# Where the first nine weight chunks are added, how the first operands are loaded, and what the schedule counts for a transfer's issue

## The chip, the core and the metric

The kernel runs on one core of one Trainium2 chip. The metric is the device time of one execution in microseconds, the median of several runs. A core has four engines that compute here: PE (TensorE, matmuls; PEld is its loading of weights), DVE (VectorE), ACT (ScalarE) and POOL (GpSimd). SP (SyncE) only issues transfers, which 16 transfer engines carry out. Each engine takes its instructions from one queue, in order.

## The reference

Attention over 4 batches of 8 heads (576 positions, 64 per head), with a mask by blocks of 64 positions, feeds a first layer and that a second one. The inputs q, k and v are float32; the weights arrive as float64.

```python
scores = scale * np.matmul(q, k.transpose(0, 1, 3, 2))
mask = block_i >= block_j                      # blocks of 64
scores = np.where(mask, scores, -1000000000.0)
attn = np.exp(scores - np.max(scores, axis=-1, keepdims=True))
attn = attn / (np.sum(attn, axis=-1, keepdims=True) + 1e-09)
out = np.matmul(attn, v)
...
x = out.transpose(0, 2, 1, 3).reshape(2304, 512)
h = np.maximum(np.maximum(x @ w1, x @ w2), x @ w3)     # 512 -> 768
x = h @ w_out                                          # 768 -> 512
h = np.maximum(x @ w_in, 0.0)                          # 512 -> 2048
return h * h @ w_out                                   # 2048 -> 512
```

## The kernel before

**Attention.** Two heads make a pair, four pairs a batch, 16 pairs in all. The 576 positions are split into a first group of 256 query rows and a second of 320. For the first batch (pairs 0 to 3) the first group is done for all four pairs first, so that the first layer can begin early; its operands lie in one tile `zk` of 128x3x256: the queries of each head, padded with zeros to 128 rows (`z`, two slices), and the keys (`k`). `score_operands_f32` loads these three slices with three transfers, in the order z of head 0, k, z of head 1. For the tile of rows i (i is 0 or 1 in the first group) the names run: scores `sc_i`, masked with a memset; their row maxima `nm` (a reduction on DVE, then a small scaling); `P`, the exponentials with their row sums `sm`, on ACT; transposes `tp` on PE; a copy `ta` of them; the product with the values, `av`; reciprocals of the sums, spread by PE (`r`) and copied (`rs`); the scaled result split into a high part `xh` and a low part `xl`. The third group of operands belongs to pair 2, here called the third pair.

**Weights.** A weight of 64 bits is read as two 32-bit words, low and high, side by side in a tile `raw_w` of 128x512x2. `load_w_` makes a float32 `f_w` of one chunk (128x512) in steps: ACT scales the high words; ACT scales the low words to an integer; DVE shifts, then combines with the sign (`scalar_tensor_tensor`); GpSimd adds the two as 32-bit integers; ACT rounds to the high part `w1h`; DVE subtracts to get the low part `w1l`. The first layer has 18 chunks `w_c_i` (c is a block of 128 of its 768 columns, i one of w1, w2, w3), its second weights 6 (`wo1`). The chunks are numbered in the order in which they are recorded; `chunks` holds the names so far, the present one included. For a few chunks the place of `f_w` is the raw tile itself, and the rows then say `raw_w<-raw_w`.

**Products.** Each product of the first layer, `l`, is a sum of three matmuls: `xh` by `w1l`, `xl` by `w1h`, `xh` by `w1h`. The second layer does the same in another form, with weights written out to memory once and read back (`woh`, `wol`, `wq`).

**What sets the order.** All work is only recorded at first, in `Plan.note`. `Plan.issue` then goes through the recorded instructions with a clock of its own: for each engine it knows when the engine is free and when each instruction's operands are there, and it always takes the instruction that can start first (of several, the one of the lowest rank, then the earliest recorded), and writes it into that engine's queue. So the costs in `duration`, `transfer`, `SEM` and `LAP` set the order in every queue, SP's too. For a transfer the costs are: an issue holds SP for 60 ns, and the bytes pass a queue, at a fixed rate, that opens 1,500 ns after the issue. As all instructions are written by one helper, nearly all rows have line L187, and are told apart by the names of their tiles.

Of the kernel before, what the change touches and what calls it, by code (L numbers as in the profile page):

```python
# [17 lines left out]
ALU = mybir.AluOpType  # L18
# [6 lines left out]
NPAIR = H // 2  # L25
# [15 lines left out]
GA, GB = 256, 320  # L41
# [127 lines left out]
class Plan:  # L169
# [56 lines left out]
    def issue(self):  # L226

        ops, free, held, queue = self.ops, self.free, self.held, self.queue
        left = [0 for op in ops]
        users = [[] for _ in ops]  # L230
        for op in ops:
            for d in (*op.deps, *op.after):
                if d.end is None:
                    left[op.index] += 1
                    users[d.index].append(op)
        waiting = {e: {} for e in free}

        def offer(op):
            for e in op.engines:
                when = 0.0  # L240
                for d in op.deps:
                    when = max(when, d.end + ((SEM[d.engine] + (500 if e == 'pe' else 0)) if d.engine != e else 0))
                waiting[e][op.index] = when, shares_port(e, op)

        for op in ops:
            if not left[op.index]:
                offer(op)
        for _ in ops:
            best = None
            for e, w in waiting.items():  # L250
                if not w:
                    continue
                other = held["pool" if e == "dve" else "dve"] if e in held else 0.0
                start = {i: max(free[e], at, other if port else 0.0) for i, (at, port) in w.items()}
                t = min(start.values())
                i = min((i for i, s in start.items() if s <= t), key=lambda i: (ops[i].rank, i))
                if best is None or t < best[0]:
                    best = t, e, i
            t, e, i = best
            op = ops[i]  # L260
            op.engine = e
            length = duration(e, op) * SLOW[e]
            if e in held and waiting[e][i][1]:
                held[e] = t + length - HOLD[e]
            for other in op.engines:
                del waiting[other][i]
            if e == "sp":
                queue = max(t + 1500, queue) + transfer(op)
                op.end, free[e] = queue + 400, t + 60
            else:  # L270
                op.end = t + length
                free[e] = op.end - LAP[e]
            for tile in op.makes:
                tile.make()
            self.tc.keep_in_program_order(self.call(self.real[e], alias(e, op.name), op.args, op.kw))
            for u in users[i]:
                left[u.index] -= 1
                if not left[u.index]:
                    offer(u)
        self.ops, self.queue = [], queue  # L280
# [15 lines left out]
def width(x):  # L296
    return math.prod(x.area.shape[1:])


def alias(engine, name):  # L300
    return {"act": "copy", "dve": "tensor_copy"}.get(engine, name) if name in ("copy", "tensor_copy") else name


def shares_port(engine, op):
    if engine not in ("dve", "pool"):
        return False
    sources = [x for k, x in op.kw.items() if k.startswith("in") and isinstance(x, View) and not x.psum]
    if engine == "pool" or len(sources) > 1:
        return bool(sources)
    return bool(sources) and not op.kw["out"].psum and width(op.kw["out"]) % 2 == 0 and op.name != "tensor_reduce"  # L310
# [31 lines left out]
def transfer(op):  # L342
    x = next(v for v in op.views())
    return 128 * 4 * width(x) / 320.0


@with_exitstack
def fused_kernel(ctx: ExitStack, tc: tile.TileContext, z0, k0, qk, v, w123, wo1, win2, wo2, out):
    nc = Plan(tc)
    mm = nc.tensor.matmul  # L350

# [25 lines left out]
    def load_w(src, hi, lo, name):  # L377
        with nc.ranked(CFG["PC"]):
            load_w_(src, hi, lo, name)

    def load_w_(src, hi, lo, name, f=None):
        spare = SPARE[len(chunks)] if len(chunks) < len(SPARE) else "."
        chunks.append(name)
        if spare in "hl":
            both = m1.tile([128, 512, 3], U32, tag="h" + spare, name=f"raw_{name}").rearrange("p n t -> p (n t)")
            raw, f = both[:, :1024].rearrange("p (n t) -> p n t", t=2), both[:, 1024:].bitcast(F32)
        elif spare == "r":
            raw = at.tile([128, 512, 2], U32, tag="raw", bufs=CFG["RB"], name=f"raw_{name}")
            f = m1.tile([128, 512], F32, tag="xf", bufs=4, name=f"f_{name}")
        else:  # L390
            raw = m1.tile([128, 512, 2], U32, tag="wraw", bufs=2, name=f"raw_{name}")
            if f is None:
                f = m1.tile([128, 512], F32, tag="wf", bufs=2, name=f"f_{name}")
        nc.sync.dma_start(out=raw, in_=src.bitcast(U32).rearrange("p (n t) -> p n t", t=2))
        low, high = raw[:, :, 0], raw[:, :, 1]
        fi, qi = f.bitcast(I32), low.bitcast(I32)
        if pat(CFG["A1"] if len(chunks) <= 24 else CFG["A2"]):
            nc.vector.tensor_scalar(out=f, in0=high.bitcast(F32), scalar1=2.0 ** -112, scalar2=None, op0=ALU.mult)
        else:
            nc.scalar.activation(out=f, in_=high.bitcast(F32), func=AF.Copy, scale=2.0 ** -112)  # L400
        if pat(CFG["Q"] if len(chunks) <= 24 else CFG["Q2"]):
            nc.vector.tensor_scalar(out=qi, in0=low, scalar1=2.0 ** -29, scalar2=None, op0=ALU.mult)
        else:
            nc.scalar.activation(out=qi, in_=low, func=AF.Copy, scale=2.0 ** -29)
        nc.vector.tensor_scalar(out=fi, in0=fi, scalar1=3, scalar2=None, op0=ALU.logical_shift_left)
        nc.vector.scalar_tensor_tensor(out=fi, in0=high.bitcast(I32), scalar=-2 ** 31, in1=fi, op0=ALU.bitwise_and,
                                       op1=ALU.bitwise_or)
        if not CFG["HIS"]:
            nc.gpsimd.tensor_tensor(out=fi, in0=fi, in1=qi, op=ALU.add)
        if hi is None:  # L410
            return
        if pat(CFG["HI"]):
            nc.vector.tensor_copy(out=hi, in_=f)
        else:
            nc.scalar.copy(out=hi, in_=f)
        if CFG["HIS"] == 2:
            nc.gpsimd.tensor_tensor(out=fi, in0=fi, in1=qi, op=ALU.add)
        elif CFG["HIS"]:
            nc.gpsimd.tensor_tensor(out=qi, in0=fi, in1=qi, op=ALU.add)
            f = low.bitcast(F32)  # L420
        nc.vector.tensor_tensor(out=lo, in0=f, in1=hi.bitcast(F32), op=ALU.subtract)

    w1, wo1_t = {}, {}
    chunks = []
# [4 lines left out]
    def pat(p):  # L429
        return p > 0 and len(chunks) % p == 0 or p < 0 and len(chunks) % -p != 0  # L430
# [55 lines left out]
    def score_operands_f32(n, g):  # L486


        a, w = GROUPS[g] if n < NPAIR else (0, S)
        if n < NPAIR and g == 0:  # L490
            zk = at.tile([128, 3, GA], F32, tag="tb", bufs=2 * CFG["TB"][1], name=f"zk{n}")
            z, k = [zk[:, h] for h in range(2)], zk[:, 2]
        else:
            z = [at.tile([128, w], F32, tag=t, bufs=CFG["QB"][2 * (t == "kl")], name=f"z{n}_{t}") for t in ("qs", "kl")]
            k = at.tile([128, S], F32, tag="kh", bufs=CFG["QB"][1], name=f"k{n}")
        nc.sync.dma_start(out=z[0], in_=z0[n, :, 0, a:a + w])
        nc.sync.dma_start(out=k, in_=k0[n, :, :a + w])
        nc.sync.dma_start(out=z[1], in_=z0[n, :, 1, a:a + w])
        return [[(z[h], k)] for h in range(2)], None

    def value_operands(n, g):
# [279 lines left out]
    with nc.behind(marks[CFG["WO"]][0]), nc.ranked(2):  # L781
        for m in (m for q in range(NQ) for m in (q, q + NQ)):
            t = at.tile([128, 2, DM], F32R, tag="wos", name=f"wos{m}")
            load_w_(wo2[128 * m:128 * m + 128, :], t[:, 0], t[:, 1], f"wo_{m}")
            nc.sync.dma_start(out=wo_d[m], in_=t.bitcast(F32))
# [20 lines left out]
    def second_rows(q):  # L806
        f = forms_f[q] = w2p.tile([128, 8, 256], F32, tag="wqf", name=f"wqf{q}")
        load_w_(win2[q + NQ], None, None, f"wi_{q + NQ}", f[:, 0:2].rearrange("p i n -> p (i n)"))
# [240 lines left out]
```

## Time and profile before

| | |
|---|---|
| median of 3 runs | 888.12 us (883.44 to 889.05) |
| the profiled execution | 888.7 us, of which its span 886.9 us |
| mean granted clock of TensorE | 0.995 |
| PE busy | 864.2 us (97% of the span), 5464 matmuls |
| DVE busy | 601.1 us (68%) |
| ACT busy | 424.9 us (48%) |
| POOL busy | 104.0 us (12%), 94 instructions |
| moved by transfers | 157.73 MB, mean 178 GB/s |

The span is the time from the first to the last instruction on the core. An engine's busy time leaves out waits and the issuing of transfers. Matmuls are pipelined, so a full PE shows as busy all the time. [...] A row of a stage gives its start and end, its length, the busy time of each engine with the number of its instructions in brackets, the mean granted clock, the mean busy share of the transfer engines and the rate of the transfers.

### The profile page before, as it was taken

The numbers are of one execution on the slowest core, as the hardware profiler recorded it, in microseconds if no ns is written. First come the engines' busy times: TensorE is split into PE (matmuls) and PEld (weight loads), VectorE is DVE, ScalarE is ACT, GpSimd is POOL, SyncE is SP. The second block draws the span as 40 slices with busy tenths as digits, with TensorE's granted clock in tenths as the row PEclk, the third lists the DMA queues.
The fourth block names the chain that finished last, engine by engine and source line by source line (L and its number), as shares of the span: only waits on it lengthen the run. The fifth ranks groups of instructions, "written<-read, shape, count | busy, mean of one in ns | idle before, by whom it ended". The sixth has DMA issues, their size and how long they took to land.

```text
span 886.9 us, 14852 instructions
## 1 busy us (share of the span) xinstructions
PE 864.2 (97%) x5464; PEld 777.7 (88%) x5464; DVE 601.1 (68%) x1376; ACT 424.9 (48%) x1016; POOL 104.0 (12%) x94
## 2 busy tenths in 40 slices
PE   5899999999999999999999989999999999999997
PEld 4567799998999989899999979898999989999896
DVE  6998678878788988646557766546755457544543
ACT  6888667667688787544555231113211114211111
POOL 2233200000001111214442230000000000000000
PEclk9999999999999999999999999999999999999999
DMA  8745432232255563554656578454765536655221
GB/s 294 237 138 174 131 114 89 85 115 86 85 184 177 175 213 118 196 190 165 257 203 237 164 299 338 160 230 168 270 229 184 207 145 229 215 200 196 72 72 71
DMA packets 52056, 157.73 MB, mean 178 GB/s; under 512 B 8592, under 2 KB 16016, under 8 KB 48400
## 3 DMA queue, kind: packets, MB, share of 16 engines
q1 hardware_dynamic: 51984, 156.78, 50.5%
q8 instruction: 43, 0.70, 0.3%
q14 instruction: 29, 0.24, 0.1%
HBM read 124.26 MB, written 32.51 MB: 177 GB/s over the span
## 4 chain that ended last, share of the span: by engine, by line
PE 92%; DVE 2%; DMA 2%; ACT 2%; issue 0%; POOL 0%; SPq 0%; ACTq 0%; POOLq 0%; DVEq 0%
PE l L187 34%; PE acc L187 22%; PE ph_x L187 11%; PE ph_y L187 8%; PE av L187 5%; PE sc L187 5%; PE tp L187 4%; PE sc_t L187 2%; DMA raw_wi<-in_win 1%; PE tp_t L187 1%; DMA raw_wo<-in_wo 1%; DMA zk<-in_k 1%; PE r L187 0%; ACT P L187 0%; DVE f_wo L187 0%
## 5 line engine op out<-in xcount | busy, mean ns | idle before, releaser
L187 PE MATMUL acc<-woh,g 128*128 128x512 f32 x576 | 198.5, 395 | 0.0
L187 PE MATMUL l<-xh,w1l 128*128 128x256 f32 (+1 forms) x576 | 174.3, 303 | 0.9 <-DVE run L187 0.9
L187 PE MATMUL l<-xl,w1h 128*128 128x256 f32 (+1 forms) x576 | 172.2, 299 | 0.0
L187 PE MATMUL l<-xh,w1h 128*128 128x256 f32 (+1 forms) x576 | 172.2, 299 | 0.0
L187 ACT CAST g<-c 128x384 fp32r<-128x384 f32 x96 | 49.3, 513 | 220.8 <-DVE c L187 220.8
L187 PEld LDWEIGHTS acc<-woh,g 128*128 128x128 f32 x576 | 108.5, 189 | 19.4
L187 PE MATMUL acc<-wol,g 128*128 128x512 f32 x288 | 113.3, 393 | 0.0
L187 PEld LDWEIGHTS l<-xh,w1l 128*128 128x128 f32 x576 | 109.0, 189 | 4.1 <-issue 1.5
L187 PEld LDWEIGHTS l<-xl,w1h 128*128 128x128 f32 x576 | 109.1, 189 | 2.6 <-issue 1.7
L187 PEld LDWEIGHTS l<-xh,w1h 128*128 128x128 f32 x576 | 109.1, 189 | 1.9 <-issue 1.2
L187 PE MATMUL ph_x<-t,wq 128*128 128x384 f32 x432 | 87.7, 337 | 2.7 <-ACT p L187 2.7
L187 PEld LDWEIGHTS ph_x<-t,wq 128*128 128x128 f32 x432 | 77.4, 188 | 8.9 <-ACT p L187 3.1
L187 DVE TENSOR_TENSOR g<-c,g 128x384 fp32r<-128x384 f32 x96 | 53.6, 560 | 43.0 <-ACT g L187 42.6
L187 ACT ACTIVATE P<-sc,nm 128x128 f32<-128x128 f32 (+3 forms) x128 | 66.9, 530 | 9.9 <-DVE nm L187 8.4
L187 DVE TENSOR_TENSOR run<-l,run 128x256 f32<-128x256 f32 (+1 forms) x96 | 43.7, 455 | 27.9 <-PE l L187 26.3
L187 POOL TENSOR_TENSOR f_wo<-f_wo,raw_wo 128x512 int32<-128x512 int32 x22 | 29.8, 1357 | 276.5 <-DVE sm L187 180.3
L187 PEld LDWEIGHTS acc<-wol,g 128*128 128x128 f32 x288 | 54.3, 189 | 7.8
L187 PE MATMUL l<-hh,wo1l 128*128 128x256 f32 (+1 forms) x192 | 57.7, 306 | 2.2 <-DVE wo1l L187 2.1
L187 PE MATMUL ph_y<-b,wq 128*128 128x384 f32 x288 | 58.3, 337 | 0.0
L187 PE MATMUL l<-hl,wo1h 128*128 128x256 f32 (+1 forms) x192 | 57.5, 301 | 0.0
L187 PE MATMUL l<-hh,wo1h 128*128 128x256 f32 (+1 forms) x192 | 57.4, 300 | 0.0
L187 DVE TENSOR_REDUCE nm<-sc 128x2 f32<-128x256 f32 (+2 forms) x96 | 55.1, 588 | 0.8
(135 smaller groups left out, 1613.1 us busy)
## 6 DMA issues: line engine op xcount, KB each, us to landing
wq<-wq_d SPq DMA_DIRECT2D x20, 1792.0 KB, 8.6
wq_d<-wq SPq DMA_DIRECT2D x8, 1792.0 KB, 7.7
raw<-in_qk SPq DMA_DIRECT2D x24, 576.0 KB, 3.8
wol<-wo_d SPq DMA_DIRECT2D x48, 256.0 KB, 3.2
woh<-wo_d SPq DMA_DIRECT2D x48, 256.0 KB, 4.8
raw_wo<-in_wo SPq DMA_DIRECT2D x22, 512.0 KB, 3.8
raw_w<-in_w SPq DMA_DIRECT2D x18, 512.0 KB, 5.0
wo_d<-wos SPq DMA_DIRECT2D x16, 512.0 KB, 3.1
```

Source lines behind the costliest of these rows:

```text
L187: return getattr(engine, op_name)(*map(value, args), **{k: value(x) for k, x in kw.items()})
```

## The change

There are three edits. The addition of the first nine chunks is put on DVE in place of GpSimd; the later ones stay. The host lays out the first operands of pairs 0 to 3 as one array `zk0`, and one transfer of 384 KB fills the tile `zk` in place of three of 128 KB. In the schedule an issue now holds SP for 430 ns in place of 60, and the bytes of transfers issued in the first 6 us of its own clock count 1.4 times.

```diff
-            if e == "sp":
-                queue = max(t + 1500, queue) + transfer(op)
-                op.end, free[e] = queue + 400, t + 60
+            if op.name == "dma_start":
+                queue = max(t + 1500, queue) + transfer(op) * (1.4 if t < 6000 else 1)
+                op.end, free[e] = queue + 400, t + 430
...
-            nc.gpsimd.tensor_tensor(out=fi, in0=fi, in1=qi, op=ALU.add)
+            (nc.vector if len(chunks) < 10 else nc.gpsimd).tensor_tensor(out=fi, in0=fi, in1=qi, op=ALU.add)
...
-        nc.sync.dma_start(out=z[0], in_=z0[n, :, 0, a:a + w])
-        nc.sync.dma_start(out=k, in_=k0[n, :, :a + w])
-        nc.sync.dma_start(out=z[1], in_=z0[n, :, 1, a:a + w])
+        if n < NPAIR and g == 0:
+            nc.sync.dma_start(out=zk, in_=zk0[n])
+        else:
+            nc.sync.dma_start(out=z[0], in_=z0[n, :, 0, a:a + w])
+            nc.sync.dma_start(out=k, in_=k0[n, :, :a + w])
+            nc.sync.dma_start(out=z[1], in_=z0[n, :, 1, a:a + w])
...
+    zk0 = np.stack([z0[:NPAIR, :, 0, :GA], z0[:NPAIR, :, 1, :GA], k0[:NPAIR, :, :GA]], axis=2)
```

The schedule places every queue anew. SP's queue before, where the operands of the third pair (`zk_129`) and of the fourth are issued, behind those of the second groups (`z_qs`, `k`, `z_kl`) and two tiles `kt` and `zt`:

```order
L187 DMA k_110<-in_k 128x576
L187 DMA z_kl<-in_z 128x320 x2
L187 DMA kt_116<-in_k 128x576
L187 DMA zt_118<-in_z 128x2x64
L187 DMA zk_129<-in_z 128x256
L187 DMA zk_129<-in_k 128x256
L187 DMA zk_129<-in_z 128x256
```

The same stretch of SP's queue after, with the third pair's operands in `zk_124`:

```order
L187 DMA k_116<-in_k 128x576
L187 DMA zk_124<-in_zk 128x768
L187 DMA z_kl<-in_z 128x320 x2
L187 DMA kt_137<-in_k 128x576
L187 DMA zt_141<-in_z 128x2x64
L187 DMA zk_180<-in_zk 128x768
```

The third pair's transfer moved ahead of four transfers that it stood behind; the fourth pair's is still behind them.

ACT's queue before, from its start: the loading of a table, a warm-up, then the conversion of the first chunk (`raw_w_0_0`) and the first pair's `P`:

```order
L360 ACT_TABLE_LOAD
L360 ACTIVATE warm<-warm 128x1
L187 ACTIVATE raw_w_0_0_86<-raw_w_0_0_86 128x512
L187 ACTIVATE P_0_0_138,sm_0_139<-sc_0_0_120,nm_0_127 128x128 x2
L187 ACTIVATE P_1_0_149,sm_0_139<-sc_1_0_122,nm_1_135 128x256 x2
L187 ACTIVATE raw_w_0_0_86<-raw_w_0_0_86 128x512
```

ACT's queue after, from its start:

```order
L360 ACT_TABLE_LOAD
L360 ACTIVATE warm<-warm 128x1
L187 ACTIVATE P_0_0_119,sm_0_120<-sc_0_0_100,nm_0_110 128x128 x2
L187 ACTIVATE raw_w_0_0_84<-raw_w_0_0_84 128x512
L187 ACTIVATE P_1_0_135,sm_0_120<-sc_1_0_105,nm_1_122 128x256 x2
L187 ACTIVATE raw_w_0_0_84<-raw_w_0_0_84 128x512
```

The first half of the first pair's `P` moved ahead of the conversion of the first chunk; the second half stays behind it.

DVE's queue before, ahead of the third pair's row maxima (`nm_0_294`); `f_w_1_1` is the fifth chunk:

```order
L187 TENSOR_TENSOR w1l_202<-f_w_0_2_229,w1h_188 128x512
L187 TENSOR_SCALAR f_w_1_1_259<-f_w_1_1_259 128x512
L187 TENSOR_TENSOR w1l_286<-f_w_1_0_249,w1h_275 128x512
L187 MEMSET sc_0_0_279 64x2x64
L187 MEMSET sc_1_0_281 64x2x64
L187 TENSOR_REDUCE nm_0_294<-sc_0_0_279 128x2
```

DVE's queue after, the same place, with the maxima in `nm_0_282`; a row named ISA is an addition:

```order
L187 TENSOR_TENSOR w1l_178<-f_w_0_2_210,w1h_169 128x512
L187 ISA f_w_1_0_225<-raw_w_1_0_94,f_w_1_0_225 128x1024
L187 TENSOR_SCALAR f_w_1_1_246<-f_w_1_1_246 128x512
L187 TENSOR_TENSOR av_0_249<-av_0_249,rs_0_254 128x256
L187 SCALAR_TENSOR_TENSOR f_w_1_1_246<-raw_w_1_1_96,f_w_1_1_246 128x512
L187 TENSOR_TENSOR w1l_268<-f_w_1_0_225,w1h_264 128x512
L187 TENSOR_TENSOR xl_0_205<-av_0_249,xh_0_200 128x256
L187 ISA f_w_1_1_246<-raw_w_1_1_96,f_w_1_1_246 128x1024
L187 TENSOR_TENSOR w1l_268<-f_w_1_1_246,w1h_264 128x512
L187 MEMSET sc_0_0_276 64x2x64
L187 TENSOR_REDUCE nm_0_282<-sc_0_0_276 128x2
```

The fourth and fifth additions now stand in this queue (three more are ahead of these rows), and the combining and the low part of the fifth chunk moved ahead of the third pair's maxima.

## Rows read from the trace of the kernel before

**Rows 1.** Stages: length, busy us of PE, PEld, DVE, ACT, POOL; clock, DMA, GB/s.
```profile
0.00:10.00 10.00, 4.49 (x13) 3.36 (x14) 2.83 (x9) 3.91 (x12) 0.70 (x6) 1.00 0.78 248
10.00:20.00 10.00, 6.91 (x49) 4.33 (x47) 8.40 (x22) 8.70 (x23) 4.20 (x3) 1.00 0.99 350
20.00:30.00 10.00, 7.34 (x40) 5.08 (x42) 9.84 (x28) 7.25 (x25) 2.60 (x2) 1.00 0.83 272
30.00:40.00 10.00, 9.51 (x75) 6.39 (x71) 9.71 (x26) 9.75 (x24) 2.94 (x3) 1.00 0.54 156
```

**Rows 2.** Timeline of TensorE: start, us, instruction, [idle before <-what ended it].
```profile
3.51 2.90 PE L187 MATMUL sc<-zk 128*128 128x128 f32 x8 [3.51 <-DMA zk<-in_k]
...
20.63 2.86 PE L187 MATMUL sc<-zk 128*128 128x128 f32 x16 [1.96 <-DMA zk<-in_k]
...
25.77 0.68 PE L187 MATMUL tp<-ident,P 128*128 128x128 f32 x2 [1.63 <-ACT P L187]
...
27.29 0.36 PE L187 MATMUL l<-xh,w1l 128*128 128x256 f32 x1
```

**Rows 3.** Timeline of ScalarE, its start.
```profile
7.57 0.66 ACT L187 ACTIVATE raw_w<-raw_w 128x512 f32<-128x512 f32 x1 [5.35 <-DMA raw_w<-in_w]
8.14 0.35 ACT L187 ACTIVATE P<-sc,nm 128x128 f32<-128x128 f32 x1
```

**Rows 4.** Timeline of VectorE, 0 to 45 us.
```profile
5.65 0.17 DVE L187 MEMSET sc<- 64x128 f32 x1 [4.79 <-PE sc L187]
...
8.27 0.43 DVE L187 TENSOR_SCALAR raw_w<-raw_w 128x512 int32<-128x512 int32 x1 [0.67 <-ACT raw_w L187]
...
10.76 0.17 DVE L187 MEMSET sc<- 64x128 f32 x1 [1.35 <-PE sc L187]
...
19.18 1.02 DVE L187 TENSOR_SCALAR f_w<-f_w 128x512 int32<-128x512 int32 x1
...
21.18 1.73 DVE L187 TENSOR_TENSOR w1l<-f_w,w1h 128x512 fp32r<-128x512 f32 x1
...
24.09 1.00 DVE L187 TENSOR_REDUCE nm<-sc 128x2 f32<-128x256 f32 x2
...
38.20 1.45 DVE L187 SCALAR_TENSOR_TENSOR f_w<-raw_w,f_w 128x512 int32<-128x512 int32 x1
...
43.09 0.69 DVE L187 TENSOR_TENSOR w1l<-f_w,w1h 128x512 fp32r<-128x512 f32 x1
43.70 0.21 DVE L187 TENSOR_SCALAR sm<-sm 128x1 f32<-128x1 f32 x1
...
43.94 1.04 DVE L187 TENSOR_SCALAR sm<-sm 128x5 f32<-128x5 f32 x1
```

**Rows 5.** Timeline of GpSimd, two of its additions.
```profile
18.62 1.30 POOL L187 TENSOR_TENSOR f_w<-f_w,raw_w 128x512 int32<-128x512 int32 x1 [2.62 <-ACT rs L187]
...
21.06 1.29 POOL L187 TENSOR_TENSOR f_w<-f_w,raw_w 128x512 int32<-128x512 int32 x1 [1.15 <-ACT w1h L187]
```

**Rows 6.** VectorE's groups by form, 0 to 110 us: count | busy us, mean ns | idle before.
```profile
L187 DVE SCALAR_TENSOR_TENSOR raw_w<-raw_w 128x512 int32<-128x512 int32 x6 | 4.1, 684 | 0.0
...
L187 DVE TENSOR_REDUCE nm<-sc 128x2 f32<-128x512 f32 x4 | 2.7, 683 | 0.0
L187 DVE TENSOR_SCALAR raw_w<-raw_w 128x512 int32<-128x512 int32 x6 | 2.5, 420 | 0.7 <-ACT raw_w L187 0.7
...
L187 DVE TENSOR_REDUCE nm<-sc 128x2 f32<-128x256 f32 x4 | 1.6, 396 | 0.0
```

**Rows 7.** Two later stages with a stop, columns as in the first group.
```profile
100.00:120.00 20.00, 18.18 (x137) 16.32 (x132) 14.31 (x39) 11.65 (x31) 1.30 (x1) 0.91 0.31 102
500.00:550.00 50.00, 47.30 (x238) 43.11 (x237) 33.87 (x60) 15.61 (x28) 12.46 (x12) 0.97 0.85 321
```

**Rows 8.** The chain of waits, around 51 us: start, us, what.
```profile
51.28 4.38 PE l L187 x35
```

**Rows 9.** Timeline of TensorE, the first of the later stops.
```profile
106.13 0.39 PE L187 MATMUL l<-hh,wo1l 128*128 128x256 f32 x1 [1.71 <-DVE wo1l L187]
```

More of the change, by code (lines that the diff above doesn't have):

```diff
@@ L347, in fused_kernel @@
 @with_exitstack
-def fused_kernel(ctx: ExitStack, tc: tile.TileContext, z0, k0, qk, v, w123, wo1, win2, wo2, out):
+def fused_kernel(ctx: ExitStack, tc: tile.TileContext, z0, zk0, k0, qk, v, w123, wo1, win2, wo2, out):
     nc = Plan(tc)
@@ L1037 @@
     arrays = {
-        "z0": z0, "k0": k0, "qk": qk, "v": vc, "w123": w123, "wo1": w["moe_w_out"], "win2": win2, "wo2": w["moe2_w_out"],
+        "z0": z0, "zk0": zk0, "k0": k0, "qk": qk, "v": vc, "w123": w123, "wo1": w["moe_w_out"], "win2": win2, "wo2": w["moe2_w_out"],
     }
```

## The prediction

> **What bounds the kernel now.** I read the busy time by stages first, then the timelines of TensorE, ScalarE, VectorE and GpSimd over the first 50 us, then the groups of VectorE's instructions, and last the stages with a stop later on.
>
> The stages say where anything is to be had [rows 1]. From 30 us on TensorE is busy 9.5 us and more in each ten; before that it is busy 4.49, 6.91 and 7.34 us of ten, so 11.3 us are lost by 30 us. VectorE is the engine that is full there: 9.84 and 9.71 us of ten between 20 and 40 us. The transfer engines are full between 10 and 20 us (0.99). Later there is one stop between 100 and 120 us and one between 500 and 550 us [rows 7].
>
> TensorE's stops in the head have different ends [rows 2]. The first matmul waits for its operands until 3.51; the third pair's scores wait 1.96 us for their transfer, until 20.63; the transposes at 25.77 wait 1.63 us for ScalarE's P, which waited for VectorE's row maxima (24.09, [rows 4]). The first product of the first layer runs at 27.29. The next sixteen such scores took 2.86 us, so eight cost 1.43; the first eight took 2.90, because operands were still landing.
>
> ScalarE's first real instruction is the conversion of weight chunk 0, which waits 5.35 us for its transfer, until 7.57 [rows 3]. P of the first pair stands behind it and starts at 8.14, though VectorE had begun its maxima at 5.65 [rows 4].
>
> **The change, part by part.**
>
> *Operands in one transfer.* For pairs 0 to 3, three issues of 128 KB become one of 384 KB. Bytes stay the same; eight issues go from SyncE's queue. Scores can no longer start on a third of the operands. If the one transfer lands between 3.5 us (as the first third did) and 5.0 us, the eight matmuls end between 4.9 and 6.4, against 6.41: 0 to 1.5 us earlier. I take 0.7, for a landing near 4.3. What hides it is nothing: all wait for it.
>
> *Order of ScalarE.* P of pair 0 now stands ahead of chunk 0's conversion (the order shows it). VectorE's two gaps behind this wait, 0.67 us at 8.27 and 1.35 us at 10.76 [rows 4], are 2.0 us; the second half of pair 0's P still stands behind the conversion, so I take half, 1.0 us; bounds 0 and 2.0. One copy of 128x256, 0.4 us by the reduction of that size [rows 6], goes from VectorE to ScalarE. Start together: 0.7 + 1.0 + 0.4 = 2.1 us to VectorE's good, bounds 0.4 to 3.9.
>
> *Nine additions on VectorE.* The trace has no such addition on VectorE. The nearest rows are the two-operand instructions on 128x512 words of the same strided raw tile, 684 ns [rows 6]; in a packed queue the next starts before the end (43.09 takes 0.69 us, the next begins at 43.70, [rows 4]), so each takes 0.61 us of the queue. The order lists the new instruction as 128x1024 over 512 words, so in half words; if each half word took a step of its own, the two reductions, 396 ns at 256 and 683 ns at 512 columns a half each, give 1.12 ns a column and 683 + 512 x 1.12 = 1,257 ns [rows 6]. I take 0.61, because data and operands are those of the 684 ns row: 9 x 0.61 = 5.5 us added; at 1.26 it is 11.3. Below 0.61 nothing in the rows goes for two full operands.
>
> *Waits beside GpSimd that end.* While GpSimd's addition of 18.62 runs, a VectorE instruction that takes 420 ns takes 1.02 us (19.18); beside that of 21.06 one of 684 ns takes 1.73 (21.18); later 1.45 for 0.68 (38.20) and 1.04 (43.94) for the 0.21 of its neighbour of the same kind (43.70) [rows 4 to 6]. That is 0.60 + 1.05 + 0.77 + 0.83, some 3.2 us that the nine additions cost VectorE though another engine did them. All four go.
>
> VectorE up to 46 us: -2.1 + 5.5 - 3.2 = +0.2 us; it comes out even. The gain has to come from TensorE being fed sooner within that.
>
> *What TensorE sees.* The third pair's transfer now stands ahead of four others on SyncE that it stood behind, so the 1.96 us wait is gone as a wait. What is late next is VectorE: by the new order its queue holds five additions ahead of the third pair's maxima. Up to there: 24.09 - 2.1 + 5 x 0.61 - 1.65 (the first two waits) = 23.4; and the masking and the low part of the fifth chunk, w_1_1, 2 x 0.61 = 1.2 us, now stand ahead of them too: 24.6. So the maxima come at 23.4 to 24.6, about as before, with 1.2 us of weight work already done; TensorE, which then also finds the third pair's row sums ahead of its first product, is some 1.0 us ahead at 27 to 28 us (bounds -1 and +3). From there it is its own bound: from 51.28 it has 35 products in a row, 4.4 us of stock [rows 8], so the last four additions (4 x 0.61 - 1.6 = +0.8 us of VectorE) need not reach it. The first later stop ends at 106.13 on VectorE's last slice of the second weights [rows 9]; that slice comes behind the same run of work and moves with it.
>
> *Planner.* Counting 430 ns for an issue changes no work, only the order. Past 110 us the orders differ in places where TensorE is never idle; I count nothing, and both bounds are the two later stops below.
>
> Sum: the profiled execution, 886.9 us of span and 1.8 around it, 888.7 in all, less 1.0 is 887.7; it lies 0.6 above the median of the runs, so the forecast is 888.1 - 1.0 = **887.1 us**. A measurement of this kernel tells about 1% (8.9 us) from no change.
>
> **Rivals.**
>
> *The additions run at one half word a step (slower).* 9 x (1.26 - 0.61) = 5.9 us more on an engine with 0.3 us free in ten; 887.1 + 5.9 = 893.0, or 890.4 if the stock of products hides the last four. It decides from 0.72 us an addition (0.61 + 1.0/9), where the lead is used up. For it: the order's 128x1024, and an instruction form that no row shows. Against: the operands are the same bytes. Chance 0.18. [...]
>
> *The later stops close (faster).* [...] At 500 to 550 us it is 2.70 idle and 0.97 of clock, 50 x 0.03 = 1.5: 4.2 [rows 7]. If another order leaves work for one: 887.1 - 3.6 = 883.5; both: 879.3. For it: both hang on a few instructions of VectorE and ScalarE. Against: the new order has the same run of work ahead of the first stop, and the order of the second weights is much the same. One 0.13, both 0.06.
>
> *The gain is swallowed.* If the second weights' chain does not move, TensorE reaches 104 us earlier and waits longer: 888.1. Chance 0.15. That the planner's cost does nothing is out: the orders differ from the first row.
>
> **How the numbers follow.** Forecast (886 to 889) 0.48, the rivals 0.18, 0.19, 0.15. Range: from one later stop closed with a start at its better bound (881) to a half word a step (892); it leaves out both stops closed and the far end of the slower case, about 2 in 10 with what I did not think of. Faster by over 1% (under 879.2) needs both stops and more: 0.08. Slower by over 1% (over 897) needs the dear addition and a new stop: 0.06. Within 1%: 0.86.
>
> **What would show it.** VectorE's additions at 0.68 us and none of its instructions stretched before 45 us; P of pair 0 before 7 us; no wait of the third pair's scores on a transfer; first product between 26 and 28 us; TensorE's idle time up to 30 us at 10.3 instead of 11.3. Wrong it would be with additions over 0.72 us, a first product past 28 us, or later stops that are gone or larger.

## The result, and the profile after

The changed kernel takes 895.43 us (median of 4 runs, 892.98 to 898.28), the kernel before 887.04 us beside it (4 runs, 883.44 to 889.05). The ratio is 1.0105 with a 95% interval of 1.0076 to 1.0134: slower by about 1%, where 887.1 us and no measurable change were forecast, and above the range of 881 to 892 us. The profiled execution of the changed kernel took 898.28 us (the slowest of its four), its span 896.5 us, 9.6 us more than before. TensorE is busy 869.7 us of it, so it stands idle for 26.8 us in place of 22.7.

The stages of the changed kernel, columns as in [rows 1]:

```profile
0.00:10.00 10.00, 4.78 (x16) 3.59 (x17) 3.56 (x13) 4.42 (x12) 0.70 (x6) 1.00 0.78 267
10.00:20.00 10.00, 5.31 (x30) 3.01 (x29) 7.69 (x19) 7.84 (x21) 0.00 (x0) 0.96 1.01 372
20.00:30.00 10.00, 6.93 (x34) 5.13 (x34) 8.68 (x23) 5.99 (x17) 0.00 (x0) 0.67 0.81 273
30.00:40.00 10.00, 10.00 (x59) 6.38 (x57) 7.74 (x25) 7.99 (x26) 0.00 (x0) 0.85 0.26 71
...
100.00:120.00 20.00, 17.54 (x126) 15.59 (x124) 13.12 (x35) 12.47 (x34) 4.40 (x3) 0.83 0.48 144
500.00:550.00 50.00, 45.34 (x239) 42.29 (x238) 32.98 (x55) 13.53 (x24) 13.34 (x12) 0.93 0.69 243
```

Beside [rows 1] and [rows 7] three things are new. VectorE is no longer full in the head: 8.68 and 7.74 us of ten where it had 9.84 and 9.71. TensorE's granted clock, which the profile gives as a share of its full speed, is at 0.67 and 0.85 between 20 and 40 us, where it was at 1.00. And both later stages with a stop have become worse, in idle time and in clock.

How much the clock takes can be read in the stretches in which the trace has TensorE's granted clock at 0.50 or 0.51. First the changed kernel's, then those of the kernel before (the one at the very end left out):

```profile
19.30:26.10 6.80, 5.26 (x24) 3.74 (x24) 5.72 (x13) 4.57 (x10) 0.00 (x0) 0.50 0.97 347
29.50:32.90 3.40, 3.40 (x10) 2.19 (x9) 2.62 (x13) 2.70 (x9) 0.00 (x0) 0.51 0.45 117
111.50:118.30 6.80, 6.34 (x26) 5.85 (x27) 4.24 (x12) 4.17 (x14) 0.00 (x0) 0.50 0.42 109
521.10:527.90 6.80, 5.05 (x14) 4.59 (x15) 4.17 (x9) 3.65 (x7) 1.99 (x2) 0.50 1.02 415
```

```profile
107.50:110.90 3.40, 3.40 (x18) 3.40 (x18) 0.76 (x1) 0.59 (x2) 0.00 (x0) 0.50 0.51 126
520.50:523.90 3.40, 3.40 (x10) 2.83 (x10) 2.88 (x5) 0.51 (x1) 2.64 (x3) 0.50 0.39 130
```

In the first of these stretches eight scores take 2.93 us (at 22.77, below), where sixteen took 2.86 at a clock of 1.00 [rows 2], so 1.43 for eight: 2.0 times as long. In the third the matmuls `l` of 128x256 start 0.21 us apart (114.90 to 118.10), right after it 0.12 (118.31 to 118.90): 1.8 times. As an estimate from the first ratio, half of TensorE's busy time in these rows is lost: (5.26 + 3.40 + 6.34 + 5.05) / 2 = 10.0 us after, 3.4 us before. With 4.1 us more of idle time and 6.6 us more at the lower clock that is 10.7 us, against 9.6 us in the span; the 1.1 us between them are not traced further (with 1.8 for the ratio the 6.6 us are 5.9). Of the 6.6 us the head has (5.26 + 3.40) / 2 = 4.3, the later stops 2.3. Of the 4.1 us of idle time the first 50 us have 1.5 and the two later stops 2.6. So in these two executions the head lost 5.8 us and the two later stops 4.9, nearly as much.

TensorE's timeline after:

```profile
3.97 2.93 PE L187 MATMUL sc<-zk 128*128 128x128 f32 x8 [3.97 <-DMA zk<-in_zk]
...
17.49 0.44 PE L187 MATMUL tp<-ident,P 128*128 128x128 f32 x2 [3.06 <-ACT P L187]
...
20.44 1.12 PE L187 MATMUL r<-ident,sm 128*64 128x128 f32 x8 [1.53 <-DVE sm L187]
...
22.77 2.93 PE L187 MATMUL sc<-zk 128*128 128x128 f32 x8
28.33 0.33 PE L187 MATMUL tp<-ident,P 128*128 128x128 f32 x1 [2.63 <-ACT P L187]
...
34.01 0.39 PE L187 MATMUL l<-xh,w1l 128*128 128x256 f32 x1
...
111.90 0.58 PE L187 MATMUL l<-hh,wo1l 128*128 128x256 f32 x1 [2.40 <-DVE wo1l L187]
...
522.85 0.80 PE L187 MATMUL acc<-woh,g 128*128 128x512 f32 x1 [4.66 <-DVE g L187]
```

The first product comes at 34.01 us; in [rows 2] it came at 27.29. The stop of [rows 9] is 2.40 us for 1.71. The third pair's scores no longer wait for a transfer (22.77, no wait shown), but they start 2.1 us later than with the wait. What they stand behind is the second pair's chain, and that one was held up on ScalarE and on VectorE. ScalarE's timeline:

```profile
6.21 0.37 ACT L187 ACTIVATE P<-sc,nm 128x128 f32<-128x128 f32 x1 [3.99 <-DVE nm L187]
...
13.65 0.67 ACT L187 ACTIVATE raw_w<-raw_w 128x512 f32<-128x512 f32 x1
...
14.92 0.68 ACT L187 ACTIVATE raw_w<-raw_w 128x512 int32<-128x512 uint32 x1
...
15.74 0.69 ACT L187 ACTIVATE f_w<-raw_w 128x512 f32<-128x512 f32 x1
16.31 0.67 ACT L187 ACTIVATE raw_w<-raw_w 128x512 int32<-128x512 uint32 x1
16.86 0.49 ACT L187 ACTIVATE P<-sc,nm 128x256 f32<-128x256 f32 x1
```

The first pair's P starts at 6.21, earlier than the 8.14 of [rows 3]. But the second half of the second pair's P comes only at 16.86, and TensorE waits 3.06 us for it. On ScalarE the conversions of the second and third chunk (four rows) stand ahead of it. On VectorE its row maxima are late too, with weight work between their reduction and their scaling:

```profile
14.53 0.68 DVE L187 TENSOR_REDUCE nm<-sc 128x2 f32<-128x512 f32 x1
...
15.79 0.68 DVE L187 SCALAR_TENSOR_TENSOR raw_w<-raw_w 128x512 int32<-128x512 int32 x1
16.39 0.16 DVE L187 TENSOR_SCALAR nm<-nm 128x2 f32<-128x2 f32 x1
```

P needs the scaling, which ends at 16.55 behind the shift and the combining of the second chunk. So by these rows an earlier place in ScalarE's queue alone would bring P forward by 0.3 us at most, and an earlier scaling alone by nothing: weight work stands ahead of P in both queues. The third pair in VectorE's timeline:

```profile
26.19 0.69 DVE L187 TENSOR_TENSOR w1l<-f_w,w1h 128x512 fp32r<-128x512 f32 x1 [0.68 <-ACT w1h L187]
26.90 0.17 DVE L187 MEMSET sc<- 64x128 f32 x1
27.10 0.42 DVE L187 TENSOR_REDUCE nm<-sc 128x2 f32<-128x256 f32 x1
```

The third pair's first eight scores end at 25.70 (22.77 + 2.93), against about 22.06 in [rows 2] (20.63 and half of 2.86): they start later and run while the clock is at 0.50. The low part of the fifth chunk waits for ScalarE, and the masking ahead of the maxima stands behind it until 26.90, another 1.2 us. So the maxima come at 27.10, against 24.09 in [rows 4], and more of that lies with the late and slow scores than with VectorE's queue. TensorE's 2.63 us at 28.33 run from the end of the scores; these 1.2 us are part of them. The additions show no trouble; VectorE's groups by form, 0 to 110 us, columns as in [rows 6]:

```profile
L187 DVE CUSTOM_DVE_ANT_0 f_w<-raw_w,f_w 128x1024 uint16<-128x1024 uint16 x5 | 3.4, 683 | 0.1
...
L187 DVE CUSTOM_DVE_ANT_0 raw_w<-raw_w 128x1024 uint16<-128x1024 uint16 x4 | 2.7, 687 | 0.2 <-ACT raw_w L187 0.2
```

### The profile page after: what moved, and what is told of

It is laid out like the page before. It is cut to its first block, busy times and chain, and to the rows that moved or that the text cites. A ratio compares the mean times of both kernels' runs of the same rounds, so it can differ in the third digit from the quotient of the medians.

```text
span 896.5 us, 14818 instructions
## 1 busy us (share of the span) xinstructions
PE 869.7 (97%) x5464; PEld 780.6 (87%) x5464; DVE 605.2 (68%) x1384; ACT 422.7 (47%) x1017; POOL 92.7 (10%) x85
## 4 chain that ended last, share of the span: by engine, by line
PE 91%; DMA 3%; DVE 2%; ACT 2%; issue 1%; SPq 0%; POOL 0%; POOLq 0%; DVEq 0%; ACTq 0%
PE l L187 33%; PE acc L187 22%; PE ph_x L187 11%; PE ph_y L187 8%; PE av L187 5%; PE sc L187 5%; PE tp L187 4%; PE sc_t L187 2%; DMA raw_wo<-in_wo 1%; DMA raw_wi<-in_win 1%; PE tp_t L187 1%; PE r L187 1%; DMA wo_d<-wos 1%; DMA raw_w<-in_w 0%; SPq L187 0%
## 5 line engine op out<-in xcount | busy, mean ns | idle before, releaser
L187 PE MATMUL tp<-ident,P 128*128 128x128 f32 x320 | 53.2, 280 | 8.1 <-ACT P L187 8.1
```

The source lines that it names most:

```text
L187: return getattr(engine, op_name)(*map(value, args), **{k: value(x) for k, x in kw.items()})
```

## The experiments

Three theories were on record before the first runs. A: the schedule's new cost of a transfer makes an order in which attention stands behind weight work. B: the additions fill VectorE. C: the scores lose by waiting for a whole transfer. Each ratio below is to the kernel before, on the same chip; "first product" is the time of the first layer's first matmul, and the idle time and clock are TensorE's between 10 and 50 us, all from the one profiled execution.

| kernel | edit | median, us | ratio (95%) | first product, us | idle, us | clock |
|---|---|---|---|---|---|---|
| before | | 885.5 to 887.0 | 1 | 27.29 | 6.64 | 1.00 |
| changed | all three | 895.43 | 1.0105 (1.0076 to 1.0134) | 34.01 | 8.43 | 0.87 |
| E1 | changed, old schedule | 885.46 | 0.9995 (0.9977 to 1.0013) | 27.83 | 3.73 | 0.91 |
| E2 | changed, additions on GpSimd | 895.57 | 1.0102 (1.0075 to 1.0130) | 34.59 | 7.87 | 0.83 |
| E3 | changed, three transfers | 890.49 | 1.0039 (1.0021 to 1.0057) | 34.85 | 6.29 | 0.83 |
| E4 | changed, no factor 1.4 | 883.78 | 0.9980 (0.9964 to 0.9996) | 26.29 | 5.58 | 0.91 |
| E5 | before, factor 1.4 alone | 893.15 | 1.0073 (1.0058 to 1.0088) | 32.28 | 8.83 | 0.87 |
| E6 | before, 430 ns alone | 888.69 | 1.0028 (1.0017 to 1.0039) | 25.28 | 2.98 | 0.96 |
| E7 | before, same order, additions on VectorE | 886.63 | 1.0007 (0.9994 to 1.0019) | 28.79 | 7.40 | 0.96 |
| E8 | before, same order, one transfer | 888.49 | 1.0010 (0.9986 to 1.0034) | 28.07 | 6.23 | 0.96 |
| E9 | changed, factor on the first four transfers only | 888.38 | 1.0026 (1.0008 to 1.0044) | 27.87 | 5.98 | 0.91 |
| E10 | changed, factor on all but those four | 893.28 | 1.0080 (1.0053 to 1.0106) | 32.30 | 5.98 | 0.87 |
| E11 | changed, two stops filled | 892.73 | 1.0077 (1.0050 to 1.0104) | 31.80 | 5.54 | 1.00 |
| E12 | E4 with TensorE kept busy early | 883.49 | 0.9979 (0.9959 to 0.9999) | 24.75 | 3.80 | 1.00 |

**E1, the old schedule.**

```diff
-            if op.name == "dma_start":
-                queue = max(t + 1500, queue) + transfer(op) * (1.4 if t < 6000 else 1)
-                op.end, free[e] = queue + 400, t + 430
+            if e == "sp":
+                queue = max(t + 1500, queue) + transfer(op)
+                op.end, free[e] = queue + 400, t + 60
```

> The changed kernel with the schedule's cost of a transfer set back to the old one; the nine additions on VectorE and the one transfer stay. Theory A (the schedule's new cost puts the second pair's scores and exponentials behind weight work, TensorE idles and its clock falls): the first product comes at 27 to 29 us instead of 34.01, the granted clock stays at 1.00 up to 40 us, and the time is 884 to 889 us. Theory B (the additions fill VectorE): first product still past 31 us, time 892 to 897 us. Theory C (scores have to wait for the whole transfer): the first scores still start at about 4.0 us and the time stays at 892 to 897 us.

The time is that of the kernel before, with the nine additions on VectorE and the one transfer in place. The loss hangs on the schedule; the clock was not 1.00 as A had it (0.91), yet the loss is gone.

**E2, additions on GpSimd, and E3, three transfers.**

```diff
-            (nc.vector if len(chunks) < 10 else nc.gpsimd).tensor_tensor(out=fi, in0=fi, in1=qi, op=ALU.add)
+            nc.gpsimd.tensor_tensor(out=fi, in0=fi, in1=qi, op=ALU.add)
```

> The changed kernel with all additions back on GpSimd; the new cost of a transfer and the one transfer stay. Theory A: the stop of TensorE before 20 us stays, first product past 31 us, time 892 to 898 us. Theory B: with the 9 x 0.69 us taken off VectorE the first product comes at about 28 us and the time is 885 to 889 us. Theory C: as now, 893 to 897 us.

```diff
-        if n < NPAIR and g == 0:
-            nc.sync.dma_start(out=zk, in_=zk0[n])
-        else:
-            nc.sync.dma_start(out=z[0], in_=z0[n, :, 0, a:a + w])
-            nc.sync.dma_start(out=k, in_=k0[n, :, :a + w])
-            nc.sync.dma_start(out=z[1], in_=z0[n, :, 1, a:a + w])
+        nc.sync.dma_start(out=z[0], in_=z0[n, :, 0, a:a + w])
+        nc.sync.dma_start(out=k, in_=k0[n, :, :a + w])
+        nc.sync.dma_start(out=z[1], in_=z0[n, :, 1, a:a + w])
```

> The changed kernel with three transfers of 128 KB again for each of pairs 0 to 3; the new cost of a transfer and the additions on VectorE stay. Theory A: the order is another one, because three issues are counted, but the second pair's exponentials still stand behind weight work; first product at 30 to 33 us, time 890 to 896 us. Theory B: as now, 893 to 897 us. Theory C: first scores at about 3.5 us, first product at about 28 us, time 885 to 889 us.

E2 is as slow as the changed kernel, so B falls. E3 is between; its head is as late (first product 34.85, past the 30 to 33 of A too), which is against C. Its 5 us come from later on. The stop of 4.66 us at 522.85 is gone (0.17 us of idle time between 500 and 535 us), but one of 3.98 us at 400 us is new and the clock falls behind it, so this exchange gains little. What has gone without another in its place is the stop between 100 and 120 us: TensorE is busy 19.57 us there at full clock, in the changed kernel 17.54 us at 0.83. E3's stages:

```profile
100.00:120.00 20.00, 19.57 (x156) 17.33 (x155) 13.38 (x34) 13.28 (x37) 3.01 (x2) 1.00 0.41 129
...
380.00:420.00 40.00, 36.02 (x235) 35.76 (x234) 18.55 (x36) 16.89 (x33) 10.54 (x10) 0.91 0.46 155
```

Another order moves the later stops about, whatever the head does.

**E4, without the factor.**

```diff
-                queue = max(t + 1500, queue) + transfer(op) * (1.4 if t < 6000 else 1)
+                queue = max(t + 1500, queue) + transfer(op)
```

> The changed kernel without the factor 1.4 on the bytes of the first transfers; an issue still counts 430 ns, the additions and the one transfer stay. TensorE's queue has the second pair's four scores ahead of the transposes of the first pair's second half again. Theory A, if the factor is the part that does it: first product at 26 to 29 us, granted clock 1.00 up to 40 us, time 884 to 889 us. Theory A, if the 430 ns do it: first product past 31 us, 892 to 897 us. Theories B and C: 892 to 897 us.

TensorE's timeline of E4:

```profile
3.98 2.93 PE L187 MATMUL sc<-zk 128*128 128x128 f32 x8 [3.98 <-DMA zk<-in_zk]
...
7.98 1.58 PE L187 MATMUL sc<-zk 128*128 128x128 f32 x8 [0.41 <-DMA zk<-in_zk]
...
15.29 1.14 PE L187 MATMUL tp<-ident,P 128*128 128x128 f32 x4 [2.02 <-ACT P L187]
...
26.29 0.36 PE L187 MATMUL l<-xh,w1l 128*128 128x256 f32 x1
```

The second pair's scores come at 7.98, right when their transfer lands, and the first product is 7.7 us earlier than in the changed kernel. Part of that is the execution's luck: these eight scores took 1.58 us, in the changed kernel's execution the first four of that pair, at 9.28, took 1.06, so TensorE was at full rate sooner (last section), and the clock was not 1.00 up to 40 us as A had it (0.91). The median of ten executions says more: the factor is the part that costs; with 430 ns, the additions and the one transfer left in, the time is 0.2% below the kernel before.

**E5, the factor alone, and E6, 430 ns alone,** each in the kernel before.

```diff
-                queue = max(t + 1500, queue) + transfer(op)
+                queue = max(t + 1500, queue) + transfer(op) * (1.4 if t < 6000 else 1)
```

> The kernel before with nothing but the factor 1.4 on the bytes that the schedule counts in its first 6 us: no other engine, no other transfer, 60 ns for an issue. TensorE's queue gets the transposes of both halves of the first pair ahead of the second pair's scores. Theory A (the factor alone makes the loss): first product past 31 us instead of 27.29, the granted clock below 0.9 in a stage before 40 us, time 891 to 899 us. Theory A' (the factor hurts only together with 430 ns for an issue or with the additions): 885 to 889 us.

```diff
-                op.end, free[e] = queue + 400, t + 60
+                op.end, free[e] = queue + 400, t + 430
```

> The kernel before with nothing but 430 ns for an issue in the schedule. Theory A: no loss, 882 to 888 us, with the first product at 24 to 28 us, because the third pair's transfer is issued earlier. Theory D (any other order loses, since the order before was the lucky one): 890 us or more.

TensorE's timeline of E5, then that of E6:

```profile
29.66 0.83 PE L187 MATMUL tp<-ident,P 128*128 128x128 f32 x2 [5.80 <-ACT P L187]
```

```profile
396.49 0.64 PE L187 MATMUL l<-xh,w1l 128*128 128x320 f32 x1 [3.89 <-ACT run L187]
```

The factor alone loses 0.7%, as A expected: TensorE stands for 5.80 us before the third pair's transposes. The 430 ns bring the head forward (25.28), and yet 0.3% are lost. A stop of 3.89 us that the kernel before does not have stands at 396.49, with the clock at 0.91 between 380 and 420 us; the one between 500 and 550 us has gone in exchange (0.17 us of idle time, 2.70 in [rows 7]). The time is just outside what A expected and short of what D did.

**E7 and E8, the order of the kernel before kept row by row.** E7 writes the addition into VectorE's queue at the place that the schedule found on GpSimd; E8 lets the first of three issues carry everything and drops the other two.

```diff
             nc.gpsimd.tensor_tensor(out=fi, in0=fi, in1=qi, op=ALU.add)
+            nc.ops[-1].moved = len(chunks) < 10
...
-            self.tc.keep_in_program_order(self.call(self.real[e], alias(e, op.name), op.args, op.kw))
+            self.tc.keep_in_program_order(self.call(self.real["dve" if getattr(op, "moved", False) else e], alias(e, op.name), op.args, op.kw))
```

> The kernel before with the schedule's order kept, row by row: the nine additions are planned as GpSimd's, and only when written out are put into VectorE's queue at their place. This prices the additions alone. By the sum of the prediction (9 x 0.61 less 3.2 us of stretched instructions, most of it hidden) 885 to 888 us and the first product at 26.5 to 29 us; by theory B 890 to 896 us.

```diff
+        if n < NPAIR and g == 0:
+            nc.ops[-3].whole = zk, zk0[n]
+            nc.ops[-2].whole = nc.ops[-1].whole = ()
...
+            whole = getattr(op, "whole", None)
+            if whole is None:
+                self.tc.keep_in_program_order(self.call(self.real[e], alias(e, op.name), op.args, op.kw))
+            elif whole:
+                self.tc.keep_in_program_order(self.call(self.real[e], "dma_start", (), dict(out=whole[0], in_=whole[1])))
```

> The kernel before with the schedule's order kept, row by row: for pairs 0 to 3 the first of three issues carries all 384 KB, the other two are dropped. This prices the one transfer alone. By the prediction's sum 0.5 to 2 us are gained: 883 to 886 us. By theory C the first scores start 0.3 to 0.6 us later and the second pair's no sooner: 885 to 888 us.

Neither can be told from no change: 1.0007 (0.9994 to 1.0019) and 1.0010 (0.9986 to 1.0034). The additions alone cost what the sum of the prediction has them cost, nearly nothing. The one transfer alone does not gain the 0.5 to 2 us that were expected.

**E9 and E10, which transfers the factor falls on.** The schedule's clock can be printed for each landing and set beside the trace (us; before, the ends of TensorE's waits for the two are taken, 20.63 in [rows 2]; the others are issue plus landing):

```
                 second pair's operands     third pair's operands
kernel           schedule    trace          schedule    trace
before             6.4        8.4             20.1       20.6
changed            8.2        8.7             23.9       18.2
E4                 6.4        7.9             17.1       16.6
E9                 8.2        8.0             19.8       17.4
E10                6.4        8.0             21.3       16.6
```

For the changed kernel, SyncE's two issues, and after them the transfers with the time from issue to landing as the last number:

```profile
2.11 0.43 SPq L187 DMA_DIRECT2D zk<-in_zk  x1
...
11.93 0.33 SPq L187 DMA_DIRECT2D zk<-in_zk  x1
```

```profile
zk<-in_zk SPq DMA_DIRECT2D x1, 384.0 KB, 6.6
...
zk<-in_zk SPq DMA_DIRECT2D x1, 384.0 KB, 6.3
```

So the factor is right where one looks first, at the second pair (8.2 for 8.7), and 5.7 us too late at the third, because the 14 transfers that the schedule issues in its first 6 us are all counted 1.4 times, and the third pair's stands behind them in its queue.

```diff
-                queue = max(t + 1500, queue) + transfer(op) * (1.4 if t < 6000 else 1)
+                queue = max(t + 1500, queue) + transfer(op) * (1.4 if t < 1400 else 1)
```

> The changed kernel with the factor 1.4 only on the first four transfers (the first and second pair's operands, their first values, the first chunk); 430 ns, additions and the one transfer stay. The schedule's clock then still has the second pair's operands land at 8.2 us (in the changed kernel's trace at 8.7), but the third pair's at 19.8 instead of 23.9 (in that trace at 18.2). Theory A1 (the harm is the third pair believed late, with weight work put ahead of it): first product at 26 to 29 us, time 884 to 889 us. Theory A2 (the harm is the second pair behind the first pair's transposes): the stop of 3 us before the second pair's transposes stays, first product past 31 us, 891 to 896 us.

E10 has `1400 < t < 6000` in the same place.

> The changed kernel with the factor on all transfers of the first 6 us but the first four. The schedule's clock has the second pair's operands land at 6.4 us and the third pair's at 21.3. Theory A1: some of the loss stays, 888 to 894 us, first product at 28 to 32 us. Theory A2: the second pair's scores stand ahead of the transposes of the first pair's second half again, first product at 26 to 29 us, 884 to 888 us.

TensorE's timeline of E9, then that of E10:

```profile
15.70 0.44 PE L187 MATMUL tp<-ident,P 128*128 128x128 f32 x2 [3.04 <-ACT P L187]
...
24.86 0.33 PE L187 MATMUL tp<-ident,P 128*128 128x128 f32 x1 [0.51 <-ACT P L187]
...
27.87 0.36 PE L187 MATMUL l<-xh,w1l 128*128 128x256 f32 x1
```

```profile
8.09 2.93 PE L187 MATMUL sc<-zk 128*128 128x128 f32 x8 [0.36 <-DMA zk<-in_zk]
...
26.73 0.82 PE L187 MATMUL tp<-ident,P 128*128 128x128 f32 x2 [3.50 <-ACT P L187]
...
32.30 0.39 PE L187 MATMUL l<-xh,w1l 128*128 128x256 f32 x1
```

E9 keeps the second pair's stop (3.04 us), as A2 had it, but the third pair's shrinks to 0.51, and 7 of the changed kernel's us come back. E10 has no such stop in the second pair and 3.50 us in the third, and stays at 893.28 (its first product, 32.30, is just past A1's 32). From E4 the third pair believed late costs 893.28 - 883.78 = 9.5 us, the second pair put back 888.38 - 883.78 = 4.6 us, both 11.6, and the third pair's lateness in the table (0.5, 2.4, 4.7 and 5.7 us for E4, E9, E10 and the changed kernel) rises in the order of the times. So A1 is the larger part. A2 is a smaller one: its stop is there in E9, but E9 also has the third pair 2.4 us late, so the 4.6 us are not the second pair's alone. These are differences of medians between whole orders, and they take in what each order does to the later stops (between 500 and 550 us TensorE is idle for 4.66 us in the changed kernel, 2.46 in E9 and 3.42 in E10). The first product of E9 is flattered by its profiled execution, in which TensorE came to full rate sooner (the second pair's first four scores took 0.61 us at 9.01, in the changed kernel's 1.06 at 9.28; last section): its second pair's transposes come 1.8 us before those of the changed kernel (15.70 and 17.49) with the same rows ahead of them in its queue.

**E11, two stops filled, and E12, TensorE kept busy early.**

```diff
+                    if j == 0 and h == 0:
+                        nc.ops[-1].pad = {(1, 1): 24, (2, 0): 20}.get((n, i), 0), ident
...
+            if getattr(op, "pad", None):
+                for _ in range(op.pad[0]):
+                    self.tc.keep_in_program_order(self.call(self.real["pe"], "transpose", (op.args[0], op.pad[1], op.pad[1]), {}))
```

> The changed kernel, its order kept; TensorE's stops of 3.06 and 2.63 us before the second and third pair's transposes are filled with 24 and 20 transposes of the identity into the bank that the real ones overwrite. They add nothing to the result. If the low clock at 20 to 40 us follows from those stops, the granted clock is 1.00 there, half of the time at the low level comes back, and the time is 890 to 893 us though the stops stay. If it has another reason, the clock stays at 0.67 and 0.85 there and the time at 894 to 898 us.

E12 is E4 with the same code at `{(1, 1): 16}`, and this ahead of the schedule:

```diff
+    idle = ps.real.tile([128, 512], F32, tag="av", bufs=BANKS["av"], name="idle")
+    for _ in range(12):
+        tc.nc.tensor.transpose(idle[:, :128], ident.tile.real, ident.tile.real)
```

> The kernel without the factor, with 12 transposes of the identity on TensorE before the first operands are there (from about 1.4 us) and 16 more in its stop before the second pair's transposes. If the slow first scores (eight in 2.93 us, where sixteen took 2.86 later) are slow because TensorE had stood idle, they take about 1.5 us now, ACT and VectorE start sooner, the granted clock stays at 1.00, and the time is 879 to 882 us. If they are slow for another reason, 882 to 885 us, as without these.

Stages of E11, columns as above, then TensorE's timeline of E12:

```profile
10.00:20.00 10.00, 7.72 (x54) 5.54 (x53) 8.00 (x21) 8.11 (x21) 0.00 (x0) 1.00 1.03 381
20.00:30.00 10.00, 7.41 (x58) 6.21 (x59) 9.01 (x24) 6.47 (x19) 0.00 (x0) 1.00 0.80 288
30.00:40.00 10.00, 10.00 (x73) 6.28 (x71) 8.92 (x27) 8.95 (x27) 0.00 (x0) 1.00 0.38 111
```

```profile
1.36 2.82 PE L382 MATMUL idle<-ident 128*128 128x128 f32 x12 [1.36 <-POOL ident masks.py:199]
4.10 1.85 PE L187 MATMUL sc<-zk 128*128 128x128 f32 x8
```

In E11 the clock stays at 1.00 where it was at 0.67 and 0.85, with the same order. The first product comes 2.2 us earlier, and the median is 2.7 us lower, as expected; since the intervals of the two ratios overlap, the clock row is the firmer evidence. E12's first scores take 1.85 us in place of 2.93 and its head is the best of all (24.75), but its time is that of E4: 883.49 against 883.78. It was expected at 879 to 882 us, and no gain over E4 can be told. What takes the head's gain back was not traced; E4's profiled execution is the slowest of its ten (886.21 us), so its head need not be the usual one. E4 and E12 lie 0.2% below the kernel before, with intervals that just leave out no change, and are the only ones of which that holds.

## Why the prediction was wrong

*The step that failed* is the planner's: "Counting 430 ns for an issue changes no work, only the order", with nothing counted for what the order costs past the head, and the 1.4 not named at all. The order was the effect. With the old costs the other two edits lose nothing (E1, 0.9995); the factor alone loses 0.7% on the kernel before (E5, 893.15 us), most of the 1%; and without it the changed kernel takes 883.78 us (E4).

*What TensorE sees* failed with it. The transfer wait of the third pair did go, and "what is late next is VectorE" held in name. But the 23.4 to 24.6 us for the third pair's maxima added up the queue's instructions as if VectorE never waited in between. The scores that the maxima need ended on TensorE only at 25.70, since the second pair's chain ahead of them had lost 3.06 and 1.53 us there; and VectorE was idle for 1.32 us of ten between 20 and 30 us, since rows ahead of the maxima waited for TensorE and ScalarE. The maxima came at 27.10, the first product at 34.01 against "27 to 28", and TensorE's idle time up to 30 us is 13.0 us, not 10.3. I compared ScalarE's queue for the first pair and not for the second, where four conversions now stand ahead of P, and VectorE's only ahead of the third pair's maxima, not of the second's.

*The clock in the head* was priced for the later stops only. New stops in the head cost, by the estimate above, 4.3 us of clock beside their idle time, and E11 shows the link: with two of them filled the clock is at 1.00 where it was at 0.67 and 0.85.

*Operands in one transfer*: the landing was right (3.97, with 4.3 taken), the gain was not. The eight first scores took 2.93 us, not 1.43, and ended at 6.90, not between 4.9 and 6.4. They are slow not because operands were still landing, as the prediction read [rows 2], but because TensorE ran slowly, for they take as long with one transfer, which had landed, and 1.85 us after 2.8 us of other work in E12. At the old order no gain from the transfer can be told (E8).

*Order of ScalarE* for the first pair, and P "before 7 us": right, 6.21.

*Nine additions and the waits that end*: right. 683 and 687 ns, by the row that was taken; no instruction on VectorE takes over 0.75 us before 50 us; 1.0007 at the old order (E7). The rival of half a word a step is out.

*The later stops* were expected to stay or close; they grew. The 3.6 us for a closed first stop were my estimate, 1.82 us of idle time and 20 x 0.09 of clock by [rows 7], and no run shows them as a gain; the changed kernel has 20 - 17.54 = 2.46 us of idle time there and a clock of 0.83, E3 0.43 us and 1.00. TensorE's 4.66 us at 522.85 end with VectorE's g, which waits for a g on ScalarE that stands behind a weight chunk, as ScalarE's timeline after shows:

```profile
519.91 0.65 ACT L187 ACTIVATE raw_wi<-raw_wi 128x512 int32<-128x512 uint32 x1 [6.26 <-DMA raw_wi<-in_win]
...
521.71 0.49 ACT L187 CAST g<-c 128x384 fp32r<-128x384 f32 x1
```

It is the same kind of loss as in the head: in one queue, weight work (here with a wait for its transfer) stands ahead of work that TensorE needs. The orders of E3 and E6 have this stop at 0.17 us and one of about 4 us near 400 us in its place, so the exchange gains little. Why one order has the one stop and not the other was not settled. No sum over the head can see what these stops cost; the one between 100 and 120 us, which E3 does not have, is most of the 5 us between E3 and the changed kernel.

## What to carry to other kernels

Where a planner writes the queues, a change to its costs is a change to every queue: compare the landing that it assumes with the landing in the trace for each transfer and not only for the first, since a factor that fits the second pair's (8.2 us for 8.7) was 5.7 us out at the third's. A sum of the instructions in a queue gives no time for the last of them unless each one's operands are followed to their own engine. The stops late in the kernel move with the order as well and are to be looked at in each trace. And a stop of TensorE in the head is to be priced with the clock as the trace has it behind the stop: here 0.50 from 19.30 to 26.10 us.

## What was not expected of the hardware

TensorE's first matmuls run at about half rate. Eight scores take 2.93 us at 4 us, where sixteen took 2.86 at 20.63 [rows 2], 1.85 after 2.8 us of other work (E12), and 1.58 at 7.98 (E4). The stage rows give the granted clock as 1.00 there all the same, so it is the durations that tell. When the rate rises differs between these executions: the second pair's eight scores took 1.58 us at 7.98 in E4 and 2.93 us at 8.09 in E10, with the same instructions ahead of them on TensorE. What raises the rate is not shown.
